# Weights split two blocks at a time, POOL normalising part of the attention weights, and a new order on TensorE, in an attention + maxout kernel

## The chip, the cores and the metric

The kernel runs on one core of a Trainium2 chip. The metric is device time in microseconds (us) of one execution; the time before is a median over three runs. The core has five engines, each of which executes its own instruction stream in order and waits on semaphores for the others: TensorE (PE in the profile; PEld is its weight load), VectorE (DVE), ScalarE (ACT), GpSimd (POOL) and SyncE (SP, which here only issues transfers).

## The reference

Sliding-window attention with a linear distance bias, then a dense maxout layer and an output projection:

```python
scores = q @ k.T / 8                                   # 8 batches, 8 heads, 576 positions, head size 64
scores = where(0 <= i - j < 128, scores - slope[h] * |i - j|, -1e9)
attn   = exp(scores - max); attn /= attn.sum(-1) + 1e-9
x      = (attn @ v)  as 4608 tokens x 512
h      = maximum(x @ w1, x @ w2, x @ w3)               # 512 -> 768 each
out    = h @ w_out                                     # 768 -> 512
```

q, k and v are float32. The four weight matrices arrive as float64 and are given to the kernel as pairs of 32-bit words.

## The kernel before

**Attention.** The eight batches are worked through in tasks, one per batch and pair of heads (32 tasks), and each task in five steps of up to 128 query rows (160 steps). A step belongs to a pair of steps, for which the work on TensorE is issued together. `products` (line 259) multiplies q and k for two steps into the score banks; `score` masks (lines 274, 277), adds the bias and takes the row minimum on DVE (line 289), and takes exp with its row sum on ACT (line 293). `sums_of` makes the reciprocals of the row sums on DVE (lines 302, 305), `normalise` multiplies each p by them on ACT (line 312), `turn` transposes p on TensorE (line 321), ACT copies the transposes out (lines 325, 331, 334), POOL cuts them to the triangles of the window (lines 335, 339), and `mix` multiplies them with v (line 361). `turn` comes LAG_T = 4 steps behind the products, `mix` LAG_X = 6 steps.

**Dense layers.** They go by a scheme with seven products of half-size blocks in place of eight (like Strassen's). Every operand is a sum or difference of blocks, split into a high and a low part in the fp32r type (ACT casts the high part, DVE or POOL subtracts to get the low one), and each product is three matmuls: low by high, high by low, high by high. A *unit* (lines 510 to 519) is one such product: 6 matmuls of 128x288 for the first layer, 9 for the output layer. There are 11 groups per batch (nine for the maxout layer, two for the output) of seven units each, 77 units per batch. A product's result stays in one of three banks of accumulators, is copied out by ACT (line 519) or combined by DVE (lines 459 to 476), and further products are accumulated on top of it in the same bank, so that the copy must be done before the bank's next product. `factors_h` forms the differences and splits of the maxout result (DVE `sub`, line 391; ACT cast, line 387; POOL subtraction, line 388).

**Weights.** In the first batch the float64 words of each of the 12 groups of weights are converted to float32 on ACT and DVE (lines 136 to 144), four sums are made (line 158), and seven blocks of 128x256 are split into high and low part (lines 168, 169). The nine groups of the maxout layer are written to DRAM (`keep`) and from the second batch on are read back through a ring of two groups, issued from POOL's queue (line 221). The three groups of the output layer stay in SBUF (`ow`).

**Order.** Every piece of work is an event with a time in steps; `at` collects them, and they are issued in order of that time. Within a step: mix, then turn, then products, then the units due. A scheduler then orders each engine's instructions by this order and by when it takes operands to be ready, so that instructions can be pulled ahead of others. `weights` is called in each step and each unit of batch 0 and advances the preparation.

## Time and profile before

| | |
|---|---|
| median of three runs | 850.38 us (847.42 to 852.41) |
| profiled execution | 846.03 us, of which the span from first to last instruction is 844.3 us |
| PE busy | 780.3 us (92%), 6272 matmuls |
| DVE busy | 570.0 us (68%) |
| ACT busy | 544.5 us (64%) |
| POOL busy | 310.3 us (37%) |
| moved by DMA | 184.78 MB, 219 GB/s on the mean |

Busy time counts an engine as busy while an instruction of its own is under way; matmuls overlap, and several in flight count once. The mean duration of a matmul in a group is therefore longer than its share of the time; the pace is read from the starts of the groups in the timeline. In the timeline, a row is a stretch of like instructions on one engine: start, duration, engine, line, operation, tiles, shape, count, and in brackets idle time ahead of it with what ended it. In the windows view each stretch has, for each engine, busy us with the number of instructions, then the granted clock of TensorE as a share of full speed, the DMA share, and GB/s.

### The profile page before, as it was taken

How to read it: one execution, taken by the hardware profiler on the slowest of the kernel's cores; microseconds unless marked ns; L12 is line 12 of the kernel's file. 1: busy time of each engine (PE TensorE's matmuls, PEld its weight loads, DVE VectorE, ACT ScalarE, POOL GpSimd, SP SyncE). 2: the span in 40 equal slices, each digit the busy share in tenths (PEclk: the TensorE clock that was granted, in tenths of full speed). 3: DMA queues.
4: the chain of work that ended last, by engine and by line, in shares of the span. 5: the costliest groups of instructions: out<-in, count | busy, mean ns of one | idle time of the engine just before them, and what ended most of it. 6: DMA issues, size and time to landing. Idle time of an engine off the chain costs nothing.

```text
span 844.3 us, 17942 instructions
## 1 busy us (share of the span) xinstructions
PE 780.3 (92%) x6272; PEld 674.3 (80%) x6272; DVE 570.0 (68%) x1830; ACT 544.5 (64%) x1790; POOL 310.3 (37%) x544
## 2 busy tenths in 40 slices
PE   4767778799999999999999999999999999999997
PEld 2335666589888988888888988889888988889897
DVE  5788989996666845775557845775657846583552
ACT  6898888876666856676556756675657756642332
POOL 1212141442354415452345415451345415440431
PEclk9865989799999999999999999999999999999999
DMA  6742568673887558873787558873787557764851
GB/s 230 278 168 70 220 230 305 210 257 125 262 277 249 195 171 261 277 253 118 239 273 252 196 175 267 275 255 110 245 281 240 194 187 244 230 223 153 296 205 56
DMA packets 43401, 184.78 MB, mean 219 GB/s; under 512 B 4784, under 2 KB 13744, under 8 KB 34096
## 3 DMA queue, kind: packets, MB, share of 16 engines
q0 software_dynamic: 18144, 115.61, 41.7%
q1 hardware_dynamic: 25024, 67.97, 22.8%
q8 instruction: 49, 0.80, 0.4%
q14 instruction: 40, 0.33, 0.1%
q10 hardware_dynamic: 144, 0.07, 0.0%
HBM read 157.68 MB, written 25.95 MB: 217 GB/s over the span
## 4 chain that ended last, share of the span: by engine, by line
PE 68%; DVE 8%; issue 8%; POOL 6%; ACT 6%; DMA 3%; SPq 0%; POOLq 0%; ACTq 0%; DVEq 0%
PE ps_m L510 53%; PE ps_x L361 6%; PE ps_s L259 5%; PE pt L321 4%; POOL hs L388 3%; DMA wt<-keep 2%; POOL pp L339 1%; POOL pp L335 1%; ACT p L293 1%; ACT hs L387 1%; DVE hs L158 1%; DVE t L473 1%; DMA hs<-in_w_all 1%; DVE hs L144 1%; DVE xs L388 1%
## 5 line engine op out<-in xcount | busy, mean ns | idle before, releaser
L510 PE MATMUL ps_m<-xs,wt 128*128 128x288 f32 x3024 | 440.8, 302 | 19.9 <-DVE hq L476 7.6
L510 PEld LDWEIGHTS ps_m<-xs,wt 128*128 128x128 f32 x3024 | 414.6, 191 | 46.6 <-issue 12.2
L519 ACT COPY t<-ps_m 128x288 f32<-128x288 f32 x264 | 101.2, 392 | 92.3 <-PE ps_m L510 91.9
L335 POOL TENSOR_SCALAR_AFFINE_SELECT pp<-pr 128x256 f32<-128x256 f32 (+1 forms) x128 | 53.9, 421 | 263.0 <-ACT pr L334 175.9
L510 PE MATMUL ps_m<-hs,ow 128*128 128x288 f32 x1008 | 144.5, 299 | 3.2 <-POOL hs L388 2.4
L293 ACT ACTIVATE p<-s,st 128x128 f32<-128x128 f32 (+1 forms) x320 | 126.7, 399 | 27.9 <-DVE st L289 27.2
L510 PEld LDWEIGHTS ps_m<-hs,ow 128*128 128x128 f32 x1008 | 136.0, 188 | 9.6 <-POOL hs L388 5.9
L388 POOL TENSOR_TENSOR hs<-hq,hs 128x288 fp32r<-128x288 f32 x112 | 101.3, 914 | 88.3 <-ACT hs L387 88.1
L221 POOL DMA_DIRECT2D wt<-keep x126 | 69.8, 554 | 150.3 <-PE ps_m L510 148.8
L312 ACT ACTIVATE p<-p,st 128x128 f32<-128x128 f32 (+1 forms) x320 | 108.6, 399 | 20.6 <-DVE st L305 20.0
L289 DVE CUSTOM_DVE_ANT_0 s<-ps_s,bias 128x128 f32<-128x128 f32 (+1 forms) x300 | 77.5, 283 | 25.9 <-PE ps_s L259 19.0
L473 DVE TENSOR_TENSOR t<-ps_m,t 128x288 f32<-128x288 f32 x144 | 65.1, 453 | 43.5 <-PE ps_m L510 27.3
L361 PE MATMUL ps_x<-pp,v 128*64 128x256 f32 (+3 forms) x768 | 85.6, 338 | 7.3 <-POOL pp L335 6.6
L277 DVE COPY_PREDICATED ps_s<-prev,ps_s 128x256 f32<-128x256 uint8 x120 | 50.6, 421 | 56.9 <-PE ps_s L259 55.7
L259 PE MATMUL ps_s<-qk 64*64 64x192 f32 (+1 forms) x1080 | 71.3, 346 | 11.5 <-DVE st L289 7.4
L321 PE MATMUL pt<-ident,p 128*128 128x128 f32 (+1 forms) x320 | 62.0, 295 | 17.3 <-ACT p L312 15.2
L387 ACT CAST hs<-hq 128x288 fp32r<-128x288 f32 x120 | 50.3, 433 | 39.0 <-DVE hq L474 26.0
L361 PEld LDWEIGHTS ps_x<-pp,v 128*64 128x64 f32 (+1 forms) x768 | 46.7, 140 | 35.1 <-POOL pp L335 11.8
L321 PEld LDWEIGHTS pt<-ident,p 128*128 128x128 f32 (+1 forms) x320 | 37.2, 145 | 42.7 <-ACT p L312 20.9
L474 DVE TENSOR_TENSOR hq<-t,hq 128x288 f32<-128x288 f32 x144 | 67.4, 475 | 2.7
L259 PEld LDWEIGHTS ps_s<-qk 64*64 64x64 f32 x1080 | 40.1, 141 | 26.9 <-issue 13.2
L293 ACT ACTIVATION_READ_ACCUMULATOR p<-s,st 128x1 f32 (+1 forms) x320 | 61.5, 192 | 0.0
(56 smaller groups left out, 719.2 us busy)
## 6 DMA issues: line engine op xcount, KB each, us to landing
wt<-keep POOLq DMA_DIRECT2D x63, 1024.0 KB, 7.2
wt<-keep POOLq DMA_DIRECT2D x63, 768.0 KB, 4.6
qk<-in_qk SPq DMA_DIRECT2D x31, 576.0 KB, 5.8
hs<-in_w_all SPq DMA_DIRECT2D x24, 512.0 KB, 6.6
v<-in_v SPq DMA_DIRECT2D x32, 320.0 KB, 4.8
keep<-wt SPq DMA_DIRECT2D x9, 1024.0 KB, 4.7
outT<-t SPq DMA_DIRECT2D x64, 144.0 KB, 1.8
keep<-wt SPq DMA_DIRECT2D x9, 768.0 KB, 5.2
```

The source lines that it names most:

```text
L221: nc.gpsimd.dma_start(wts[n, a], keep[n % 9][a])
L259: nc.tensor.matmul(ps[j][d:d + D, o:o + k1 - k0], lhsT=qkt[t][j * D:(j + 1) * D, 0, q0:q0 + D], rhs=qkt[t][j * D:(j + 1) * D, 1, k0:k1], s ...
L289: nc.vector.tensor_tensor_reduce(out=s[:n], in0=ps[j][:n, P:2 * P], in1=(bias if i else bias0)[:n, 2 * hp + j, :], scale=-0.125, scalar=3. ...
L293: nc.scalar.activation(p[:n, j], s[:n], AF.Exp, bias=st[:n, 0, a, j:j + 1], scale=-1.0, accum_out=st[:n, 1, a, j:j + 1])
L312: nc.scalar.activation(p[:n, j], p[:n, j], AF.Copy, scale=st[:n, 2, a, j:j + 1])
L321: nc.tensor.transpose(out=pt[:, a, j, :n], in_=p[:n, j], identity=ident[:n, :n])
L361: nc.tensor.matmul(x[j * D:(j + 1) * D, c:c + e - a], lhsT=vv[:n, i, j * D:(j + 1) * D], rhs=w[:n, j].rearrange("p a b -> p (a b)")[:, a:e ...
L388: e.tensor_tensor(out=lo, in0=src, in1=hi.bitcast(F32), op=ALU.subtract)
L473: nc.vector.tensor_tensor(out=s, in0=ps, in1=e, op=ALU.add)
L474: nc.vector.tensor_tensor(out=h, in0=s, in1=h, op=ALU.max)
L510: nc.tensor.matmul(ps, lhsT=lt, rhs=rt, start=i == 0 and k in (0, 1, 4), stop=i == len(pairs) - 1, skip_group_check=True,)
L519: nc.scalar.copy(out=e, in_=ps)
```

## The change

Five things change, and nothing that is computed.

1. *Splitting of weights.* The four sums are written so that two neighbouring blocks lie behind each other; blocks 0 and 1, 2 and 3, and 4 and 6 are then split with one ACT cast and one DVE subtraction of 128x512 each, block 5 alone with 128x256. So 84 casts and 84 subtractions become 48 and 48 (36 of twice the width). `ow` becomes one tile in place of seven. The pace of the preparation goes from 2 of 10 pieces per call to 1.4 of 7.
2. *Normalising.* In the first two batches every other p is normalised by one POOL multiplication of 128x256 in place of two ACT instructions of 128x128: 20 POOL instructions more and 40 ACT instructions fewer.
3. *Attention order.* Within a step the work is issued as mix, products, turn instead of mix, turn, products, and mix and products stand at the head of the step.
4. *Differences.* In `factors_h`, the differences that are formed last are issued two or five units later.
5. *Pinning.* From step 50 on, matmuls and transposes keep on TensorE the order in which they are issued; the scheduler no longer moves them there.

```diff
-    ow = [const.tile([P, 3, 2, W], F32R, name=f"ow{k}") for k in range(7)]
+    ow = const.tile([P, 7, 3, 2, W], F32R, name="ow")
...
-            (s1, a10, a11, ALU.add), (s2, s1, a00, ALU.subtract), (s4, a01, s2, ALU.subtract),
-            (s3, a00, a10, ALU.subtract),
+            (h0[:, a], l0[:, a], l0[:, b], ALU.subtract), (l0[:, b], l0[:, b], l1[:, b], ALU.add),
+            (h1[:, a], l0[:, b], l0[:, a], ALU.subtract), (h1[:, b], l1[:, a], h1[:, a], ALU.subtract),
...
-    def part(g, k):
-        src = blocks(g)[k]
+    def part(g, n):
+        (l0, h0), (l1, h1) = [[x.bitcast(F32) for x in words(g, j)] for j in range(2)]
+        src = (l0, h1, l1, h0[:, :W])[n]
...
-        nc.scalar.copy(out=t[:, 0], in_=src)
-        nc.vector.tensor_tensor(out=t[:, 1], in0=src, in1=t[:, 0].bitcast(F32), op=ALU.subtract)
+        t = t[:, (slice(0, 2), slice(2, 4), slice(4 - k, 7 - k, 2), 5 - k)[n]]
+        if n < 3:
+            src = src.rearrange("p (k n) -> p k n", k=2)
+            hi, lo = t[:, :, 0], t[:, :, 1]
+        else:
+            hi, lo = t[:, 0], t[:, 1]
+        nc.scalar.copy(out=hi, in_=src)
+        nc.vector.tensor_tensor(out=lo, in0=src, in1=hi.bitcast(F32), op=ALU.subtract)
...
+    def pe(ins):
+        if fixed:
+            tc.keep_in_program_order(ins)
...
         for a, p in enumerate(two):
+            if t < 2 * NP and (t + a) % 2 == 0:
+                nc.gpsimd.tensor_tensor(
+                    out=p[:n], in0=p[:n], in1=st[:n, 2, a].unsqueeze(2).broadcast_to([n, 2, P]), op=ALU.mult
+                )
+                continue
             for j in range(2):
                 nc.scalar.activation(p[:n, j], p[:n, j], AF.Copy, scale=st[:n, 2, a, j:j + 1])
...
         elif ij == (1, 1):
             t = hq["t", p]
+            when += 2 * (p < 2)
...
             later(when, cut, 4, b10)
+            when += 5 if p < 2 else 2
             later(when, sub, b10, b10, t)
...
-                weights(2, 10 * g_order.index(g) + 4 + k)
+                weights(1.4, 7 * g_order.index(g) + 4 + (0, 0, 1, 1, 2, 3, 2)[k])
...
-                at(c + LAG_T + 0.02, turn, t * NB + i)
-                at(c + 0.03, products, t * NB + i)
+                at(c + 0.002, products, t * NB + i)
+                at(c + LAG_T + 0.003, turn, t * NB + i)
...
-            at(e - e % 2 + shift[b] + LAG_X + 0.01, mix, t, i)
+            at(e - e % 2 + shift[b] + LAG_X + 0.001, mix, t, i)
...
+    at(2 * n_steps + LAG_X + shift[2], fix)
```

What this moves is seen in the instruction streams. In these rows a line number is that of the kernel that the row belongs to: units are line 510 before and 529 after, products (tile `ps_s`) 259 and 271, transposes (`pt`) 321 and 338, mix (`ps_x`) 361 and 378.

TensorE, a pair of steps in the middle of a batch (the same place in every batch from the third on), before:

```order
L510 MATMUL ps_m_6189<-xs,wt_6040 128x288 x6
L361 MATMUL ps_x<-pp,v 64x256 x4
L510 MATMUL ps_m_6132<-xs,wt_6040 128x288 x6
L321 MATMUL pt<-ident,p 128x128 x2
L321 MATMUL pt<-ident,p 128x64 x2
L259 MATMUL ps_s<-qk 64x192 x8
L510 MATMUL ps_m_6246<-xs,wt_6068 128x288 x6
```

and now:

```order
L529 MATMUL ps_m_6091<-xs,wt_5942 128x288 x6
L378 MATMUL ps_x<-pp,v 64x256 x4
L271 MATMUL ps_s<-qk 64x192 x8
L338 MATMUL pt<-ident,p 128x128 x2
L338 MATMUL pt<-ident,p 128x64 x2
L529 MATMUL ps_m_6031<-xs,wt_5942 128x288 x6
```

The transposes now stand between the products and the units, in every pair of steps from there on; and the one unit that stood between mix and transposes here has gone behind them.

TensorE, the pair of steps ahead of that one, before:

```order
L361 MATMUL ps_x<-pp,v 64x256
L510 MATMUL ps_m_5882<-xs,wt_5809 128x288 x6
L510 MATMUL ps_m_6005<-xs,wt_5856 128x288 x6
L510 MATMUL ps_m_6016<-xs,wt_5856 128x288 x6
L510 MATMUL ps_m_6074<-xs,wt_5919 128x288 x6
L361 MATMUL ps_x<-pp,v 64x256
L361 MATMUL ps_x<-pp,v 64x128 x2
L361 MATMUL ps_x<-pp,v 64x64 x4
L321 MATMUL pt<-ident,p 128x128 x4
L259 MATMUL ps_s<-qk 64x128 x4
L259 MATMUL ps_s<-qk 64x192 x4
```

and now:

```order
L378 MATMUL ps_x<-pp,v 64x256 x2
L378 MATMUL ps_x<-pp,v 64x128 x2
L378 MATMUL ps_x<-pp,v 64x64 x4
L271 MATMUL ps_s<-qk 64x128 x4
L271 MATMUL ps_s<-qk 64x192 x4
L338 MATMUL pt<-ident,p 128x128 x4
```

The first matmul of mix no longer stands four units ahead of the others: the four units come before all of mix.

DVE, where the last difference of the first third of a batch's maxout (`hq<-hq,t`, line 391 before, 408 after) meets the first combinations of the next (lines 476 and 495), before:

```order
L391 TENSOR_TENSOR hq<-hq,t 128x288
L476 TENSOR_TENSOR hq<-ps_m_5666,t 128x288
L476 TENSOR_TENSOR hq<-ps_m_5754,t 128x288
L302 TENSOR_SCALAR st<-st 64x2
L476 TENSOR_TENSOR hq<-ps_m_5655,t 128x288
L305 RECIPROCAL st<-st 64x2
```

and now:

```order
L314 TENSOR_SCALAR st<-st 64x2
L317 RECIPROCAL st<-st 64x2
L408 TENSOR_TENSOR hq<-hq,t 128x288
L495 TENSOR_TENSOR hq<-ps_m_5560,t 128x288
L495 TENSOR_TENSOR hq<-ps_m_5652,t 128x288
L495 TENSOR_TENSOR hq<-ps_m_5549,t 128x288
```

The reciprocals of the row sums have moved ahead; the difference, which is issued later in the program, still stands ahead of the three combinations.

More of the change, by code (lines that the diff above doesn't have):

```diff
@@ L144, in convert, with sums @@
         nc.vector.tensor_tensor(out=lf, in0=lf, in1=hw, op=ALU.mult)
-    def blocks(g):
+    def sums(g):
         (l0, h0), (l1, h1) = [[x.bitcast(F32) for x in words(g, j)] for j in range(2)]
         a, b = slice(0, W), slice(W, 2 * W)
-        return l0[:, a], h0[:, b], h1[:, a], h1[:, b], l1[:, a], h0[:, a], l1[:, b], l0[:, b]
-    def sums(g):
-        a00, s1, s2, s4, a01, s3, a11, a10 = blocks(g)
         for out, x, y, op in (
-            (s1, a10, a11, ALU.add), (s2, s1, a00, ALU.subtract), (s4, a01, s2, ALU.subtract),
-            (s3, a00, a10, ALU.subtract),
+            (h0[:, a], l0[:, a], l0[:, b], ALU.subtract), (l0[:, b], l0[:, b], l1[:, b], ALU.add),
+            (h1[:, a], l0[:, b], l0[:, a], ALU.subtract), (h1[:, b], l1[:, a], h1[:, a], ALU.subtract),
         ):
             nc.vector.tensor_tensor(out=out, in0=x, in1=y, op=op)
-    def part(g, k):
-        src = blocks(g)[k]
+    def part(g, n):
+        (l0, h0), (l1, h1) = [[x.bitcast(F32) for x in words(g, j)] for j in range(2)]
+        src = (l0, h1, l1, h0[:, :W])[n]
         if g < 9:
-            if k in (0, 4):
-                place(g, k // 4)
-            t = wts[g, k // 4][:, k % 4]
-        else:
-            t = ow[k][:, g - 9]
-        nc.scalar.copy(out=t[:, 0], in_=src)
-        nc.vector.tensor_tensor(out=t[:, 1], in0=src, in1=t[:, 0].bitcast(F32), op=ALU.subtract)
-        if g < 9 and k in (3, 6):
-            nc.sync.dma_start(keep[g][k // 4], wts[g, k // 4].bitcast(F32))
+            if n in (0, 2):
+                place(g, n // 2)
+            t, k = wts[g, n // 2], n // 2 * 4
+        else:
+            t, k = ow[:, :, g - 9], 0
+        t = t[:, (slice(0, 2), slice(2, 4), slice(4 - k, 7 - k, 2), 5 - k)[n]]
[6 more added lines that the diff above has]
+        nc.vector.tensor_tensor(out=lo, in0=src, in1=hi.bitcast(F32), op=ALU.subtract)
+        if g < 9 and n in (1, 3):
+            nc.sync.dma_start(keep[g][n // 2], wts[g, n // 2].bitcast(F32))
     def place(n, a):
@@ L191, in preparing @@
             yield
-            for k in range(7):
-                while g < 9 and not ahead(g, k // 4):
+            for k in range(4):
+                while g < 9 and not ahead(g, k // 2):
                     yield True
@@ L198, in preparing @@
                 fetch(g_order[n + 2])
-    prepared = 0
+    prepared, owed = 0, 0
     steps_of_weights = preparing()
     def weights(n=0, upto=0):
-        nonlocal prepared
-        while n > 0 or prepared < upto:
+        nonlocal prepared, owed
+        owed += n
+        while owed >= 1 or prepared < upto:
             stuck = next(steps_of_weights, True)
             if stuck:
-                assert prepared >= upto or prepared == 120, (prepared, upto)
+                assert prepared >= upto or prepared == 84, (prepared, upto)
+                owed = 0
                 return
             prepared += 1
-            n -= 1
+            owed = max(0, owed - 1)
     streamed = 18
@@ L218, in stream @@
         n, a = divmod(streamed, 2)
-        if n < 9 * B and prepared == 120 and ahead(n, a):
+        if n < 9 * B and prepared == 84 and ahead(n, a):
             place(n, a)
@@ L263, in products @@
                         start=True, stop=True, skip_group_check=True,
-                    )
+                    ))
     def score(t, i):
@@ L320, in turn @@
             for j in range(2):
-                nc.tensor.transpose(out=pt[:, a, j, :n], in_=p[:n, j], identity=ident[:n, :n])
+                pe(nc.tensor.transpose(out=pt[:, a, j, :n], in_=p[:n, j], identity=ident[:n, :n]))
         r = s_p.tile([P, 2, 2, P], F32, name="pr", bufs=2)
@@ L360, in mix @@
             for j in range(2):
-                nc.tensor.matmul(
+                pe(nc.tensor.matmul(
                     x[j * D:(j + 1) * D, c:c + e - a],
@@ L509, in unit @@
         for i, (lt, rt) in enumerate(pairs):
-            nc.tensor.matmul(
+            pe(nc.tensor.matmul(
                 ps, lhsT=lt, rhs=rt, start=i == 0 and k in (0, 1, 4), stop=i == len(pairs) - 1,
                 skip_group_check=True,
-            )
+            ))
         if g < 9:
@@ L569, in attention_maxout_kernel, with fix @@
     for s in range(1, n_steps + LAG_X):
-        at(s + 0.2, weights, 2)
+        at(s + 0.2, weights, 1.4)
+    def fix():
+        nonlocal fixed
+        fixed = True
+    at(2 * n_steps + LAG_X + shift[2], fix)
     load(0)
```

7 lines of the change are left out of this document (4 added, 3 removed).

## The prediction

> **What bounds the kernel now.** I read the busy times by stretch first (us of PE, PEld, DVE, ACT and POOL, each with its instructions, then the granted clock).
>
> ```profile
> 20.00:80.00 60.00, 43.30 (x266) 21.91 (x265) 50.07 (x194) 54.41 (x183) 13.75 (x30) 0.68 0.51 184
> 80.00:200.00 120.00, 101.87 (x753) 83.97 (x752) 112.59 (x344) 97.98 (x304) 37.68 (x57) 0.89 0.65 231
> 200.00:790.00 590.00, 579.65 (x4853) 518.22 (x4852) 374.72 (x1203) 363.74 (x1223) 239.10 (x422) 1.00 0.68 224
> ```
>
> There are two kernels in one. To 200 us the weights are prepared beside the first two batches: from 20 to 80 us ACT is the fullest (54.41 of 60), from 80 to 200 us DVE (112.59 of 120), and TensorE runs at a reduced clock (0.68, 0.89). From 200 to 790 us TensorE is busy for 579.65 of 590 us at full clock while DVE, ACT and POOL have room. There only fewer or cheaper boundaries on TensorE save time. So I read its timeline next, over three pairs of steps of one batch.
>
> ```profile
> 411.21 1.08 PE L361 MATMUL ps_x<-pp,v 128*64 128x256 f32 x8
> 412.22 0.70 PE L321 MATMUL pt<-ident,p 128*128 128x128 f32 x4
> 412.86 0.88 PE L259 MATMUL ps_s<-qk 64*64 64x192 f32 x16
> 413.67 6.66 PE L510 MATMUL ps_m<-xs,wt 128*128 128x288 f32 x48
> 420.25 1.25 PE L361 MATMUL ps_x<-pp,v 128*64 128x256 f32 x16
> ...
> 430.87 0.60 PE L321 MATMUL pt<-ident,p 128*128 128x128 f32 x4
> 431.40 0.88 PE L259 MATMUL ps_s<-qk 64*64 64x192 f32 x16
> ...
> 441.25 3.47 PE L510 MATMUL ps_m<-xs,wt 128*128 128x288 f32 x24
> 444.65 0.65 PE L361 MATMUL ps_x<-pp,v 128*64 128x256 f32 x2
> 445.22 3.45 PE L510 MATMUL ps_m<-xs,wt 128*128 128x288 f32 x24
> 448.61 1.24 PE L361 MATMUL ps_x<-pp,v 128*64 128x256 f32 x14
> 449.78 0.66 PE L321 MATMUL pt<-ident,p 128*128 128x128 f32 x4
> 450.36 0.77 PE L259 MATMUL ps_s<-qk 64*64 64x128 f32 x16
> 451.07 5.86 PE L510 MATMUL ps_m<-xs,wt 128*128 128x288 f32 x42
> 456.86 1.08 PE L361 MATMUL ps_x<-pp,v 128*64 128x256 f32 x8
> 457.88 1.06 PE L510 MATMUL ps_m<-xs,wt 128*128 128x288 f32 x6
> 458.78 0.65 PE L321 MATMUL pt<-ident,p 128*128 128x128 f32 x4
> 459.35 0.88 PE L259 MATMUL ps_s<-qk 64*64 64x192 f32 x16
> 460.16 5.86 PE L510 MATMUL ps_m<-xs,wt 128*128 128x288 f32 x42
> ```
>
> From start to start, 42 unit matmuls take 5.79 us (451.07 to 456.86) and 24 take 3.40: 18 in 2.39, so 0.133 each, and 0.21 per stretch for getting in and out. The transposes between mix and products take 0.64 (412.22 to 412.86) or 0.58 (449.78 to 450.36). What they cost between units is seen once in the early part, at full clock:
>
> ```profile
> 172.56 0.27 PE L321 MATMUL pt<-ident,p 128*128 128x128 f32 x1
> 172.58 0.51 PE L510 MATMUL ps_m<-xs,wt 128*128 128x288 f32 x2
> 172.93 0.27 PE L321 MATMUL pt<-ident,p 128*128 128x128 f32 x1
> ...
> 183.01 1.19 PE L361 MATMUL ps_x<-pp,v 128*64 128x256 f32 x14
> 183.96 0.38 PE L259 MATMUL ps_s<-qk 64*64 64x192 f32 x2
> ```
>
> One transpose and two unit matmuls take 0.37 (172.56 to 172.93); less 2 x 0.133 that is 0.10 for the transpose. Transposes and units use the array in one shape (128\*128), and next to each other they pay no boundary.
>
> **The change on TensorE, from 200 us.** *Products ahead of transposes.* Four transposes beside units cost 0.42, against 0.58 to 0.64 behind mix: 0.19 saved on the mean, if mix to products costs what mix to transposes did, and products to transposes what products to units did. Per batch seven of the ten pairs have mix directly ahead: 7 x 0.19 = 1.33. Where units stand ahead (430.87 to 431.40, 0.53), the 0.11 saved comes back as the boundary between units and products: nothing. The attention of the later batches fills some 545 us from 200 us on, and a batch takes 94.5 us (the stall below comes at 333.12 and at 427.57), so 5.8 batches: 7.7 us. *Mix in one piece.* The two early mix matmuls cost 0.57 (444.65 to 445.22) and break 48 units into 24 and 24 (3.40 + 3.39 against 6.58 at 413.67, so 0.21), while the fourteen left are under way as long as sixteen elsewhere (1.24 against 1.25): 0.78. *The lone unit.* From mix to mix the piece now takes 1.02 + 0.90 + 0.57 + 0.81 + 5.79 = 9.09; in the new order 1.02 + 0.81 + 0.42 + 6.58 = 8.83: 0.26. These two come in five batches: 5.2 us. Together 12.9 us.
>
> One wait stays.
>
> ```profile
> PE ps_m L510 <- DVE hq L476: 7.0, 5, 1.4
> ...
> 333.12 3.46 PE L510 MATMUL ps_m<-xs,wt 128*128 128x288 f32 x24 [1.41 <-DVE hq L476]
> ...
> 427.57 3.46 PE L510 MATMUL ps_m<-xs,wt 128*128 128x288 f32 x24 [1.40 <-DVE hq L476]
> ```
>
> The first row is a wait of 200 to 790 us (total, times, longest): TensorE stands 1.4 us once in each of five batches, for a combination on DVE that is queued behind the last difference, which itself waits for POOL to have read its input. The change issues that difference five units later, but DVE's stream still has it ahead of the three combinations, and POOL's operations ahead of it are the same. I count nothing for it, and take 5 x 0.2 off, since what the pair of steps ahead of the stall saves is waited away there. That leaves **-12 us**. The bounds: if the boundary only moves, the first part is lost and -4 remains; if mix to products is almost free, as where fourteen mix matmuls take 0.95 (183.01 to 183.96) against 1.17, another 0.22 x 7 x 5.8 = 9 is won: -21. On the far side, ACT's copies of finished products may now stand behind exps that start earlier; a new wait of 0.2 us in each of 58 pairs would give 12 back, so 0 is the other end.
>
> By the Trainium skill ("TensorEngine Tiling (Array Packing)", section Tiling Modes) every change of tiling mode drains the array; by that rule mix to products (128x64 to 64x64) stays a paid boundary and transposes to units none. The 0.10 agrees with it; by the rule alone the sum is the -12, and -21 isn't reached.
>
> **The change up to 200 us.** The costs:
>
> ```profile
> L312 ACT ACTIVATE p<-p,st 128x128 f32<-128x128 f32 (+1 forms) x320 | 108.6, 399 | 20.6 <-DVE st L305 20.0
> L388 POOL TENSOR_TENSOR hs<-hq,hs 128x288 fp32r<-128x288 f32 x112 | 101.3, 914 | 88.3 <-ACT hs L387 88.1
> L169 DVE TENSOR_TENSOR wt<-hs,wt 128x256 fp32r<-128x256 f32 x63 | 26.8, 443 | 2.3 <-ACT wt L168 2.1
> L168 ACT CAST wt<-hs 128x256 fp32r<-128x256 f32 x63 | 25.4, 429 | 6.3 <-DVE hs L158 4.7 <-DVE hs L144 0.8 <-PE ps_x L361 0.3
> L144 DVE TENSOR_TENSOR hs<-hs 128x512 f32<-128x512 f32 x24 | 16.6, 708 | 0.6 <-ACT hs L140 0.6
> L136 ACT ACTIVATE hs<-hs 128x512 int32<-128x512 uint32 x24 | 15.8, 679 | 2.3 <-DMA hs<-in_w_all 2.3
> ```
>
> Splits on DVE: 84 x 0.425 (26.8 / 63) = 35.7 before; 36 x 0.69 (16.6 / 24) + 12 x 0.425 = 30.0 now: -5.7. On ACT 84 x 0.403 = 33.9 becomes 36 x 0.66 + 12 x 0.403 = 28.5: -5.4. Normalising takes 40 x 0.339 (108.6 / 320) = 13.6 off ACT and puts 20 x 0.80 (101.3 / 112, scaled from 288 to 256 elements) = 16 on POOL, which is busy for 51 of 180 us here. What this costs DVE:
>
> ```profile
> 408.68 0.46 DVE L474 TENSOR_TENSOR hq<-t,hq 128x288 f32<-128x288 f32 x1
> ...
> 418.78 0.81 POOL L388 TENSOR_TENSOR hs<-hq,hs 128x288 fp32r<-128x288 f32 x1 [1.62 <-ACT hs L387]
> 419.13 0.78 DVE L474 TENSOR_TENSOR hq<-t,hq 128x288 f32<-128x288 f32 x1
> ```
>
> The same DVE operation takes 0.46 alone and 0.78 beside a POOL operation. All 20 POOL operations beside such a one would add 6.4 us to DVE; I take half, as much of DVE's work reads PSUM: 3.2. DVE's net is then -2.5, ACT's -19.
>
> From 20 to 80 us lie about 25 steps, so five of the eight tasks with 13 of the 20 p, and five of the twelve weight groups: ACT loses 8.8 + 2.3, DVE nothing net. DVE's 50.07 become the fullest; filled as ACT was (0.907) they need 55: -5 at most. From 80 to 200 us DVE's net -2.5 at its filling of 0.94 gives -2.6 at most. I take **-3** of these 7.6, since here the end passes from engine to engine and a freed one often waits. The ends are -8, and +9: DVE slowed by the full 6.4 (net +0.7), and each of the 20 p held 0.4 us by another POOL operation on its path.
>
> By the Trainium skill ("GPSIMD Engine Reference", section Key points) POOL shares its SBUF interfaces with DVE and collides with DVE instructions that have two SBUF inputs, which speaks against this part. The 0.78 agrees. By the rule every weight operation beside POOL is hit, the -3 becomes about 0, and the time 838.
>
> **The sum.** 846.03 (profiled execution: span 844.3 and 1.7 around it) - 12 - 3 = 831. The profiled execution lies 4.35 under the median of the runs, so the forecast for the median is **835 us**.
>
> **Rivals.** *The boundary only moves* (-4 - 3): 843. For it: products to transposes is a change of shape too. Against: one fewer change per pair remains. *POOL's queue holds the transposes*: a p normalised on POOL stands in one in-order queue with cuts that wait for ACT.
>
> ```profile
> POOL pp L335 <- ACT pr L325: 62.7, 19, 12.5
> ```
>
> The longest such wait is 12.5 us. If half of the 20 p come 2.5 us late, the transposes, and with them the products behind them on TensorE and DVE's next scores, wait 25 us: 850.4 - 15 + 25 = 860. It decides from about 1 us per p on. Against: a transpose comes four steps behind its scores. *Everything pays* (-21 - 8, on the median): 821. *No net change*: new waits for ACT and DVE behind the pinned order give back the 12, and the early part gives nothing: 850.
>
> **How the numbers follow.** A measurement of this kernel tells about 0.5% (4.25 us) from no change: faster is under 846.1, slower over 854.6. The forecast gets 0.60 (0.57 faster, 0.03 same), the moved boundary 0.15 (0.11, 0.04), POOL's queue 0.12 (0.02 same, 0.10 slower), everything pays 0.08 (faster), no net change 0.05 (0.04 same, 0.01 slower). Together faster 0.76, same 0.13, slower 0.11. The forecast's own range is 826 to 845; with the cases on either side until two in ten are left out, 822 to 850.
>
> **What would show it.** Right: behind 200 us, rows of 16 products followed by 4 transposes, and 0.45 or less from these to the units; mix rows of 8 and 16 alone; a batch of about 92 us from stall to stall in place of 94.5, and the stall of 1.4 us still there; 200 us reached 3 us earlier with ACT clearly emptier and DVE as full. Wrong: transposes behind products that take 0.6 again, TensorE waiting for `t` of ACT's copies after each pair, or transposes that wait for POOL before 200 us.

## The result, and the profile after

The changed kernel takes **836.05 us** (median of 4 runs, 835.39 to 837.38), against 849.24 us for the kernel before (4 runs beside it, 847.42 to 852.41): a ratio of 0.9843, 95% interval 0.9808 to 0.9877, 13.2 us less. Its profiled execution took 836.26 us, span 834.6; that of before 846.03, span 844.3. So from trace to trace 9.7 us are to be explained, 3.5 fewer than from median to median.

The busy times by stretch of the kernel after (columns as in the prediction's first view):

```profile
20.00:80.00 60.00, 42.28 (x266) 21.79 (x264) 51.63 (x180) 48.01 (x151) 24.42 (x42) 0.64 0.58 199
80.00:200.00 120.00, 101.42 (x735) 84.95 (x735) 110.46 (x318) 88.86 (x252) 46.71 (x64) 0.88 0.62 222
200.00:780.00 580.00, 568.85 (x4865) 515.57 (x4863) 366.32 (x1206) 363.00 (x1231) 233.23 (x423) 1.00 0.69 229
```

ACT is emptier up to 200 us (48.01 and 88.86 against 54.41 and 97.98) and POOL fuller; DVE stays as full as it was (51.63 and 110.46 against 50.07 and 112.59). Behind 200 us TensorE is still the bound.

Two marks cut the span in three: the start of the first unit, and the start of the first output layer (tile `ow`), with which the first batch's dense layers end. The timeline of TensorE before:

```profile
74.42 3.25 PE L510 MATMUL ps_m<-xs,wt 128*128 128x288 f32 x12 [0.31 <-DVE xs L388]
...
184.84 2.68 PE L510 MATMUL ps_m<-hs,ow 128*128 128x288 f32 x18
```

and after, with the same marks, then the stalls of two neighbouring batches and the last stall:

```profile
69.98 1.68 PE L529 MATMUL ps_m<-xs,wt 128*128 128x288 f32 x6
...
186.24 2.68 PE L529 MATMUL ps_m<-hs,ow 128*128 128x288 f32 x18
...
333.11 3.46 PE L529 MATMUL ps_m<-xs,wt 128*128 128x288 f32 x24 [1.36 <-DVE hq L495]
...
425.12 3.46 PE L529 MATMUL ps_m<-xs,wt 128*128 128x288 f32 x24 [1.35 <-DVE hq L495]
...
701.25 3.47 PE L529 MATMUL ps_m<-xs,wt 128*128 128x288 f32 x24 [1.36 <-DVE hq L495]
```

The first unit starts 4.4 us earlier, yet the first output layer 1.4 us later: from the one to the other 116.3 us instead of 110.4. At the first stall both kernels stand level (333.11 against 333.12), so the 1.4 us are won back between 186 and 333. Then each batch takes 92.0 us from stall to stall (333.11 to 425.12) in place of 94.45 (333.12 to 427.57): 2.42 us in each of four batches, 9.7 in all. Behind the last stall both need the same (834.6 - 701.25 = 133.35; 844.3 - 710.93 = 133.37).

Pairs of steps from two neighbouring batches in TensorE's timeline after, with the stretch that mix used to break (438.62) and the one that held the lone unit (453.48):

```profile
400.04 1.19 PE L378 MATMUL ps_x<-pp,v 128*64 128x256 f32 x14
400.98 0.33 PE L271 MATMUL ps_s<-qk 64*64 64x128 f32 x2
401.06 0.23 PE L378 MATMUL ps_x<-pp,v 64*64 64x64 f32 x2
401.12 0.71 PE L271 MATMUL ps_s<-qk 64*64 64x128 f32 x14
401.76 0.66 PE L338 MATMUL pt<-ident,p 128*128 128x128 f32 x4
402.17 6.64 PE L529 MATMUL ps_m<-xs,wt 128*128 128x288 f32 x48
408.74 1.08 PE L378 MATMUL ps_x<-pp,v 128*64 128x256 f32 x8
409.76 0.88 PE L271 MATMUL ps_s<-qk 64*64 64x192 f32 x16
410.57 0.70 PE L338 MATMUL pt<-ident,p 128*128 128x128 f32 x4
411.20 6.67 PE L529 MATMUL ps_m<-xs,wt 128*128 128x288 f32 x48
...
428.51 0.88 PE L271 MATMUL ps_s<-qk 64*64 64x192 f32 x16
...
429.74 6.68 PE L529 MATMUL ps_m<-xs,wt 128*128 128x288 f32 x48
...
436.34 1.08 PE L378 MATMUL ps_x<-pp,v 128*64 128x256 f32 x8
...
438.16 0.70 PE L338 MATMUL pt<-ident,p 64*128 64x64 f32 x4
438.62 7.02 PE L529 MATMUL ps_m<-xs,wt 128*128 128x288 f32 x48
445.57 1.19 PE L378 MATMUL ps_x<-pp,v 128*64 128x256 f32 x14
...
453.48 1.08 PE L378 MATMUL ps_x<-pp,v 128*64 128x256 f32 x8
...
462.53 1.19 PE L378 MATMUL ps_x<-pp,v 128*64 128x256 f32 x14
```

The order is as the change says: products, transposes, units. Where the prediction saw one price for every pair there are three. With 16 mix matmuls, mix to units takes 2.13 us (400.04 to 402.17) against 2.46 before (448.61 to 451.07 in the prediction's lines). Mix runs into the products: the second mix row (64\*64) stands in the middle of the products, which have the same array shape, and the transposes need 0.41 (401.76 to 402.17). With 8 mix matmuls the same way takes 2.46 (408.74 to 411.20), as it did before (411.21 to 413.67): there the last two of the four transposes have 64 rows, and the transposes need 0.63 to the units. Where the first two have 64 rows instead (the row at 438.16 bears the shape of its first transpose, 64\*128), the transposes need 0.46, and mix to units takes 2.28 (436.34 to 438.62) against 2.45 at the same place of a batch before:

```profile
344.35 1.08 PE L361 MATMUL ps_x<-pp,v 128*64 128x256 f32 x8
...
346.80 3.47 PE L510 MATMUL ps_m<-xs,wt 128*128 128x288 f32 x24
```

TensorE's waits from 200 to 780 us (total, times, longest) are the same as before in their first place, and small otherwise:

```profile
PE ps_m L529 <- DVE hq L495: 6.8, 5, 1.4
PE ps_m L529 <- ACT t L538: 1.5, 2, 1.2
```

One small wait of each batch is gone, and the prediction doesn't speak of it. In the output layer TensorE used to stop for a result of POOL (`hs`). Before:

```profile
377.27 3.65 PE L510 MATMUL ps_m<-hs,ow 128*128 128x288 f32 x24
381.13 1.86 PE L510 MATMUL ps_m<-hs,ow 128*128 128x288 f32 x12 [0.22 <-POOL hs L388]
382.83 0.60 PE L321 MATMUL pt<-ident,p 128*128 128x128 f32 x4
```

and after:

```profile
375.94 5.13 PE L529 MATMUL ps_m<-hs,ow 128*128 128x288 f32 x36
381.00 0.88 PE L271 MATMUL ps_s<-qk 64*64 64x192 f32 x16
```

The 36 matmuls take 5.06 us to the next stretch in place of 5.56.

### The profile page after: what moved, and what is told of

It is laid out like the page before. It is cut to its first block, busy times and chain, and to the rows that moved or that the text cites. A ratio compares the mean times of both kernels' runs of the same rounds, so it can differ in the third digit from the quotient of the medians.

```text
span 834.6 us, 17886 instructions
## 1 busy us (share of the span) xinstructions
PE 769.1 (92%) x6272; PEld 672.6 (81%) x6272; DVE 560.9 (67%) x1794; ACT 528.2 (63%) x1714; POOL 326.0 (39%) x564
## 4 chain that ended last, share of the span: by engine, by line
PE 68%; DVE 12%; POOL 7%; ACT 6%; issue 5%; DMA 2%; SPq 0%; POOLq 0%; ACTq 0%; DVEq 0%
PE ps_m L529 53%; PE ps_x L378 7%; PE ps_s L271 5%; POOL hs L405 4%; PE pt L338 4%; DVE t L492 2%; ACT p L305 2%; DMA hs<-in_w_all 1%; DVE wt L173 1%; DVE hq L493 1%; DVE s L301 1%; POOL pp L352 1%; POOL pp L356 1%; DVE ps_s L289 1%; POOL p L324 1%
## 5 line engine op out<-in xcount | busy, mean ns | idle before, releaser
L529 PE MATMUL ps_m<-hs,ow 128*128 128x288 f32 x1008 | 142.7, 298 | 3.0 <-POOL hs L405 1.2
L352 POOL TENSOR_SCALAR_AFFINE_SELECT pp<-pr 128x256 f32<-128x256 f32 (+1 forms) x128 | 56.6, 442 | 208.4 <-ACT pr L351 121.7
L405 POOL TENSOR_TENSOR hs<-hq,hs 128x288 fp32r<-128x288 f32 x112 | 95.2, 858 | 89.0 <-ACT hs L404 85.3
L227 POOL DMA_DIRECT2D wt<-keep x126 | 70.1, 556 | 118.4 <-PE ps_m L529 117.6
L329 ACT ACTIVATE p<-p,st 128x128 f32<-128x128 f32 x280 | 97.1, 396 | 16.6 <-DVE st L317 16.2
L271 PE MATMUL ps_s<-qk 64*64 64x192 f32 (+1 forms) x1080 | 68.8, 337 | 8.9 <-DVE st L301 4.8
L338 PEld LDWEIGHTS pt<-ident,p 128*128 128x128 f32 (+1 forms) x320 | 35.2, 145 | 49.8 <-issue 20.7
L493 DVE TENSOR_TENSOR hq<-t,hq 128x288 f32<-128x288 f32 x144 | 70.1, 490 | 2.8
L351 ACT COPY pr<-pt 128x256 f32<-128x256 f32 x64 | 19.0, 321 | 73.7 <-PE pt L338 73.6
```

The source lines that it names most:

```text
L227: nc.gpsimd.dma_start(wts[n, a], keep[n % 9][a])
L271: pe(nc.tensor.matmul(ps[j][d:d + D, o:o + k1 - k0], lhsT=qkt[t][j * D:(j + 1) * D, 0, q0:q0 + D], rhs=qkt[t][j * D:(j + 1) * D, 1, k0:k1] ...
L329: nc.scalar.activation(p[:n, j], p[:n, j], AF.Copy, scale=st[:n, 2, a, j:j + 1])
L338: pe(nc.tensor.transpose(out=pt[:, a, j, :n], in_=p[:n, j], identity=ident[:n, :n]))
L405: e.tensor_tensor(out=lo, in0=src, in1=hi.bitcast(F32), op=ALU.subtract)
L493: nc.vector.tensor_tensor(out=h, in0=s, in1=h, op=ALU.max)
```

## The experiments

The labels stand for the kernels. "Batch 1" in an expectation is the first of the eight batches. All were timed in three rounds beside the kernel before; ratios are against it. The kernel before took 848.67 to 850.08 us beside them, so that a difference of 1 us between two rows says little. The marks are those of each kernel's trace; "batch" is the time from stall to stall, and in the three kernels with the edit of e7_diff_last, where the stall is gone, from output layer to output layer of the third to sixth batch.

| kernel | us | ratio, 95% interval | first unit | first output layer | batch |
|---|---|---|---|---|---|
| before | 849.24 | | 74.4 | 184.8 | 94.45 |
| the change | 836.05 | 0.9843 (0.9808 to 0.9877) | 70.0 | 186.2 | 92.0 |
| e1_order_only | 839.06 | 0.9863 (0.9836 to 0.9890) | 75.2 | 186.0 | 92.36, one 93.9 |
| e5_no_pin | 838.59 | 0.9886 (0.9858 to 0.9915) | 70.1 | 185.0 | 92.37, one 93.9 |
| e4_turn_first | 841.81 | 0.9917 (0.9889 to 0.9945) | 71.4 | 185.4 | 93.1 |
| e7_diff_last | 830.06 | 0.9776 (0.9743 to 0.9810) | 69.8 | 186.4 | 91.3 to 92.0 |
| e2_no_pool_norm | 840.42 | 0.9885 (0.9858 to 0.9912) | 79.7 | 188.8 | 92.0 |
| e6_pool_norm_b0 | 832.27 | 0.9806 (0.9766 to 0.9846) | 70.3 | 182.7 | 92.0 |
| e3_narrow_split | 834.64 | 0.9817 (0.9790 to 0.9844) | 72.2 | 182.0 | 92.0 to 93.5 |
| e9_pairs_narrow | 842.87 | 0.9914 (0.9880 to 0.9947) | 76.2 | 190.7 | 92 to 93.6 |
| e10_wide_early | 840.44 | 0.9889 (0.9860 to 0.9918) | 70.9 | 188.9 | 92.0 |
| e12_pace | 835.63 | 0.9849 (0.9833 to 0.9866) | 79.3 | 185.5 | 92.0 |
| e11_three | 830.43 | 0.9795 (0.9772 to 0.9817) | 73.9 | 185.3 | 90.4 to 92.1 |
| e14_wide_two | 827.76 | 0.9752 (0.9727 to 0.9777) | 70.5 | 183.5 | 90.4 to 91.3 |

A scale for the early marks: e5_no_pin has the same order on TensorE as the change up to there, and its output layer begins 1.2 us earlier. Differences of about 1 us between two traces at this mark say nothing.

### TensorE's order: e1_order_only, e5_no_pin, e4_turn_first

The order of attention alone, put into the kernel before (no fixed order behind step 50, no later differences, no split, no POOL):

```diff
-                at(c + LAG_T + 0.02, turn, t * NB + i)
-                at(c + 0.03, products, t * NB + i)
+                at(c + 0.002, products, t * NB + i)
+                at(c + LAG_T + 0.003, turn, t * NB + i)
...
-            at(e - e % 2 + shift[b] + LAG_X + 0.01, mix, t, i)
+            at(e - e % 2 + shift[b] + LAG_X + 0.001, mix, t, i)
```

> The kernel before with the attention order alone (mix, products, turn); no pinning, old weights, old normalising, old differences. Theory (the gain is TensorE's boundaries): a batch from stall to stall takes 92.8 us (92.0 as in the changed kernel plus 0.78 for the two early mix matmuls, which stay without pinning), the output layer of batch 1 begins within 2 us of the 184.8 of before, and the time is 849.2 - 1.65 x 5.8 = 840. Rival (pinning makes the gain): a batch still takes 94.4 and the time is 849.

Its stalls, from the timeline:

```profile
518.78 3.46 PE L510 MATMUL ps_m<-xs,wt 128*128 128x288 f32 x24 [1.35 <-DVE hq L476]
...
611.15 3.45 PE L510 MATMUL ps_m<-xs,wt 128*128 128x288 f32 x24 [1.34 <-DVE hq L476]
```

92.37 us apart, so the order alone gives 2.1 of the 2.42 us. The theory holds, and the rival, that fixing the order on TensorE is what pays, falls. The other side of this, the change without the fixed order:

```diff
-        if fixed:
+        if False:
```

> The change without the fixed order on TensorE behind the second batch. Theory, the fixed order is worth the 0.33 us per batch by which the order alone (92.36) fell short of the change (92.03): the two mix matmuls go ahead again, batch 92.4, 837.7 us. Rival, the later differences gave that, not the fixed order: batch 92.0, 836 us.

```profile
424.30 3.46 PE L529 MATMUL ps_m<-xs,wt 128*128 128x288 f32 x24 [1.34 <-DVE hq L495]
...
441.17 0.65 PE L378 MATMUL ps_x<-pp,v 128*64 128x256 f32 x2
...
516.67 3.45 PE L529 MATMUL ps_m<-xs,wt 128*128 128x288 f32 x24 [1.36 <-DVE hq L495]
```

The two mix matmuls go ahead of the others again and break the 48 units, and the batch is at 92.37 (424.30 to 516.67): the theory's 92.4. So mix in one piece is worth 0.34 us per batch and no more, and the later differences give nothing here. (One batch of e5_no_pin took 93.9; the granted clock was 0.89 over 15 us of it. One of e1_order_only did too, with 0.91 over 18 us.)

The change with only transposes and products exchanged again:

```diff
-                at(c + 0.002, products, t * NB + i)
-                at(c + LAG_T + 0.003, turn, t * NB + i)
+                at(c + LAG_T + 0.002, turn, t * NB + i)
+                at(c + 0.003, products, t * NB + i)
```

> The changed kernel with turn again ahead of products within a step; pinning and the rest stay. Theory (the order saves 0.19 per pair of steps with mix ahead, 1.33 a batch, and pinning the 0.78 of the early mix matmuls): a batch takes 92.0 + 1.4 = 93.4, the early part as in the changed kernel, time 836 + 8 = 844. Rival (the boundary only moves, pinning does it all): a batch takes 92.0, time 836.

```profile
427.12 2.66 PE L529 MATMUL ps_m<-xs,wt 128*128 128x288 f32 x18 [0.63 <-DVE st L317]
...
520.24 2.66 PE L529 MATMUL ps_m<-xs,wt 128*128 128x288 f32 x18 [0.61 <-DVE st L317]
```

93.12 per batch, 1.1 more than the change, where 1.4 was expected; the time 841.81. The wait is shorter here (0.63 instead of 1.35), so part of what the old order costs is hidden in the stall. Added up row by row over a batch, the stretches between one run of units and the next (mix, transposes and products) take 1.9 us more than in the change, and the output layer 0.5 more, where the wait for POOL's `hs` is back (0.19 in its row); 1.2 of these 2.4 us are saved again around the stall. So the wait for `hs` goes with products ahead of transposes. What brings POOL's result forward there isn't traced.

### The stall: e7_diff_last

The last difference, which stands ahead of the three combinations in DVE's stream, is forced behind the third of them:

```diff
-            later(when, sub, b10, b10, t)
+            later(when, last if p < 2 else sub, b10, b10, t)
...
+    combined = []
+
+    def last(out, x, y):
+        with tc.issue_after(combined[-1]):
+            sub(out, x, y)
```

(`combined` collects the additions of line 495.)

> The changed kernel with the last difference of the first two thirds of the maxout forced behind the three combinations on DVE that it stood ahead of (an order of issue on DVE, nothing else). Theory (TensorE's stall of 1.35 us per batch is that difference waiting for POOL): the stall is gone, a batch takes 90.7 us in place of 92.0, time 836 - 6.7 = 829. Rival (another wait takes its place, as for the next thirds' results): a batch takes 91.5 to 92, time 834 to 836.

The longest of TensorE's waits from 200 to 780 us in this kernel, and one of its times in the timeline:

```profile
PE ps_m L535 <- DMA wt<-keep: 4.4, 4, 1.4
```

```profile
523.22 4.23 PE L535 MATMUL ps_m<-xs,wt 128*128 128x288 f32 x30 [1.42 <-DMA wt<-keep]
```

The waits for `hq`, 6.8 us in the change, are gone, so the difference was their cause, as the prediction read it. But in this trace a batch goes from 92.0 to between 91.3 and 92.0 only: a few rows later TensorE now stands up to 1.4 us for weights that are still being read back from DRAM. The mechanism is the theory's, the period is nearer to the rival's: one wait took the place of the other.

It doesn't always do so. This trace was the slowest of its four runs (833.55; the others 828.8 to 830.2): its span is only 2.8 us below the change's (831.8), the median 6.0. And e14_wide_two, which is e6_pool_norm_b0 (92.0 a batch) with this edit, has two neighbouring output layers

```profile
369.11 2.66 PE L535 MATMUL ps_m<-hs,ow 128*128 128x288 f32 x18
...
459.49 2.66 PE L535 MATMUL ps_m<-hs,ow 128*128 128x288 f32 x18
```

90.4 us apart, and another two as well; the batch between them takes 91.3 and holds a wait of 0.76 for the weights. e11_three shows the same: 90.4 twice, and 92.1 with a wait of 1.47. So the edit is worth 1.6 us in a batch whose weights come in time. How many batches of the faster runs of e7_diff_last were of this kind isn't shown.

### POOL's share: e2_no_pool_norm, e6_pool_norm_b0

All normalising back on ACT, all else as in the change:

```diff
-            if t < 2 * NP and (t + a) % 2 == 0:
-                nc.gpsimd.tensor_tensor(
-                    out=p[:n], in0=p[:n], in1=st[:n, 2, a].unsqueeze(2).broadcast_to([n, 2, P]), op=ALU.mult
-                )
-                continue
```

> The changed kernel with all p normalised on ACT. Theory (POOL's share relieves ACT up to 75 us and slows DVE afterwards, so it is worth nothing on the whole): first unit back near 74 us, the output layer of batch 1 begins at 184 to 186 us, a batch takes 92.0 as now, time 834 to 836. Rival A (it pays): the output layer of batch 1 begins at 190, time 840. Rival B (it costs the 5.8 us lost between first unit and output layer): it begins at 181, time 831.

The two marks in its timeline:

```profile
79.70 1.81 PE L524 MATMUL ps_m<-xs,wt 128*128 128x288 f32 x6 [1.80 <-DVE xs L400]
...
188.79 2.87 PE L524 MATMUL ps_m<-hs,ow 128*128 128x288 f32 x18
```

No theory gave the shape of it. POOL's share brings the first unit 9.7 us ahead (79.70 to 69.98), far more than expected, and then costs 7 us on the way to the output layer (109.1 us here, 116.3 in the change). Net it pays 4.4 us (840.42 against 836.05), which is nearest to the rival that it pays. Then the same with POOL in the first batch alone:

```diff
-            if t < 2 * NP and (t + a) % 2 == 0:
+            if t < NP and (t + a) % 2 == 0:
```

> The changed kernel with POOL normalising in the first batch only (10 p in place of 20). With none on POOL the first unit came at 79.7 us in place of 70.0, but from there to the output layer of batch 1 it took 109 us in place of 116. Theory (POOL pays ahead of the first unit, where ACT is full, and costs behind it, where DVE is full and shares the access with POOL): first unit at 71, output layer of batch 1 at 182, time 832. Rival (the early gain is waited away later whoever normalises, since the weights set the pace there): first unit at 71, output layer at 186, time 836.

```profile
182.67 2.86 PE L529 MATMUL ps_m<-hs,ow 128*128 128x288 f32 x18
```

In its marks it is as the theory had it: the first unit stays early (70.3), the output layer comes 3.6 us earlier than in the change, and the time is 832.27. With the weights split two blocks at a time, the ten p of the first batch bring the gain, and the ten of the second batch take part of it back.

What POOL's share costs DVE is seen when the weights' operations on DVE are compared from 4 to 192 us. In the change, with POOL's own 128x256 multiplication from the grouping over the whole span:

```profile
L173 DVE TENSOR_TENSOR wt<-hs,wt 128x512 fp32r<-128x512 f32 (+1 forms) x36 | 24.0, 679 | 3.6 <-ACT wt L172 3.2
...
L155 DVE TENSOR_TENSOR hs<-hs 128x256 f32<-128x256 f32 x36 | 17.1, 475 | 0.0
...
L324 POOL TENSOR_TENSOR p<-p,st 128x256 f32<-128x256 f32 x16 | 13.3, 831 | 56.8 <-DVE st L317 43.9 <-ACT wt L172 8.7 <-DVE st L301 2.7
```

and without POOL's share (e2_no_pool_norm):

```profile
L173 DVE TENSOR_TENSOR wt<-hs,wt 128x512 fp32r<-128x512 f32 (+1 forms) x36 | 23.8, 671 | 3.9 <-ACT wt L172 3.7
...
L155 DVE TENSOR_TENSOR hs<-hs 128x256 f32<-128x256 f32 x36 | 15.8, 439 | 0.0
```

All seven groups of weight operations together are busy for 100.2 us in the kernel before, 97.7 without POOL's share and 101.3 in the change. So the wider splits save 2.5 us of DVE (4.0 in the splits themselves, 35.3 to 31.3, of which 1.5 comes back in other rows), and POOL's 20 multiplications give 3.6 us back. The narrow split beside POOL's share (e3_narrow_split) takes 103.8, so both prices come out the same the other way round. But POOL's price doesn't go by the number of its multiplications: with the ten of the first batch alone (e6_pool_norm_b0) the groups take 100.6, only 0.7 less than with twenty. So the 3.6 us by which the output layer comes earlier there isn't seen as DVE time, and the reason that the theory of e6_pool_norm_b0 gives, DVE slowed behind the first unit, isn't shown.

### The split: e3_narrow_split, e9_pairs_narrow, e10_wide_early

The change with the split of before, one block at a time:

```diff
-                weights(1.4, 7 * g_order.index(g) + 4 + (0, 0, 1, 1, 2, 3, 2)[k])
+                weights(2, 10 * g_order.index(g) + 4 + k)
...
-        at(s + 0.2, weights, 1.4)
+        at(s + 0.2, weights, 2)
```

(with `ow`, `sums` and `part` as before the change)

> The changed kernel with the weights split one block at a time, as before. Theory (5.7 us of DVE and 5.4 of ACT work saved, worth about half): the output layer of batch 1 begins at 189 in place of 186.2, time 839. Rival (two blocks at a time come late for the units that need them, and that is the loss after 75 us): it begins at 183, time 833.

```profile
181.99 2.65 PE L526 MATMUL ps_m<-hs,ow 128*128 128x288 f32 x18
```

The theory that the new split as a whole pays falls: with the one of before the output layer comes 4.2 us earlier and the time is 834.64, 1.4 less than the change, with overlapping intervals of the two ratios. (In its trace 2.1 of the 4.2 us are lost again in two batches of 93.5 and 92.6 us, the first with a granted clock of 0.89 over 16 us.) The edit also puts back the seven tiles of `ow`, the old places of the blocks and the old pace; these weren't tried apart. Why should fewer instructions cost time? Two attempts to tell. First, the pairs and their pace kept, but each pair split by two narrow instructions per engine:

```diff
-        nc.scalar.copy(out=hi, in_=src)
-        nc.vector.tensor_tensor(out=lo, in0=src, in1=hi.bitcast(F32), op=ALU.subtract)
+        each = [(hi[:, c], lo[:, c], src[:, c]) for c in range(2)] if n < 3 else [(hi, lo, src)]
+        for x, y, z in each:
+            nc.scalar.copy(out=x, in_=z)
+            nc.vector.tensor_tensor(out=y, in0=z, in1=x.bitcast(F32), op=ALU.subtract)
```

> The changed kernel with each pair of blocks split by two narrow casts and subtractions in place of one wide one, in the same pieces and at the same pace. Splitting one block at a time had brought the output layer of batch 1 to 182.0 from 186.2. Theory A (the wide instructions themselves: they stand longer in ACT's and DVE's queues ahead of what TensorE waits for): output layer of batch 1 at 182 to 183, time 834. Theory B (the pace in pieces of two blocks: more is done at once): it stays at 186 or comes later by the 5 us of work that the wide form saves, 188, time 838.

842.87, the first unit 6 us later than in the change and the output layer at 190.7: it isn't the wide instruction itself that costs. This kernel differs from the change in that instruction alone and is 4.4 us later at the output layer, so the wide instruction pays, as theory B has it, and by more than that theory's 188 and 838. What is better in e3_narrow_split can only lie in what else its edit changes. Second, wide pairs in the five groups ahead of the first unit only, one block at a time later:

```diff
-            for k in range(4):
+            for k in range(4 if n < 5 else 7):
...
-                part(g, k)
+                part(g, k) if n < 5 else part_one(g, k)
```

(`part_one` is the split of one block as before; the pace is 1.4, then 2)

> The changed kernel with two blocks at a time only in the five groups of weights that are split before the first unit, and one block at a time, at the old pace, in the seven others. Theory (the wide split pays 2 us ahead of the first unit and costs 6 behind it): first unit at 70, output layer of batch 1 at 180, time 831. Rival (the gain ahead is waited away behind the first unit, as the weights set the pace): output layer at 182, as with one block at a time everywhere, time 834.5.

840.44, the output layer at 188.9. Both theories fall: mixing the two is worse than either alone.

### The pace of the weights: e12_pace

Two pieces of preparation offered in each step instead of 1.4:

```diff
-        at(s + 0.2, weights, 1.4)
+        at(s + 0.2, weights, 2)
```

> The change, but the weights are offered two pieces of preparation in each step of attention instead of 1.4, so they stand earlier in every engine's order. Theory, the preparation of the weights sets the pace from the first unit to the first output layer: preparation ends near 172 instead of 176 us, the first output layer begins near 182 instead of 186.2, 832 us; the first unit may come up to 2 us later than 70.0. Rival, DVE's and ACT's time itself is the limit and the pieces only push scores back: first unit at 73 or later, first output layer at 186 or later, 836 to 838.

The first unit starts 9.3 us later than in the change (79.3), and the output layer (185.5) within the 1.2 us that two traces of one order differ by; the time is 835.63 against 836.05. The last split of weights starts at 175.4 us, against 176.2 in the change, not at 172. The theory that the pace of the offers holds the stage up falls; that pieces offered earlier only push the first units back is what the trace shows. It also shows that the first unit's start says little of the end of this stage.

### Together: e11_three, e14_wide_two

Three edits together, and the same without the narrow split:

```diff
-            if t < 2 * NP and (t + a) % 2 == 0:
+            if t < NP and (t + a) % 2 == 0:
...
-            later(when, sub, b10, b10, t)
+            later(when, last if p < 2 else sub, b10, b10, t)
```

(e14_wide_two; e11_three has the split of e3_narrow_split besides)

> The change with three edits together: one block at a time split (e3_narrow_split), POOL normalises in the first batch only (e6_pool_norm_b0), the last difference behind the three combinations (e7_diff_last). Theory, the three act in different places and their gains add: -1.4 - 3.8 - 6.0 from 836.05, so 825 us; first output layer at 180 us, batch 92.0. Rival, the split and the normalising relieve the same waits between 75 and 180 us, so only the larger of the two counts: 826.5 to 828, first output layer at 182.5.

> The change with POOL normalising in the first batch only and the last difference behind the three combinations, weights split two blocks at a time as in the change. Compared with e11_three only the split differs. Theory, splitting two blocks at a time costs as it did in e3_narrow_split: 1.4 us above e11_three, 826.3, first output layer at 182.7. Rival, two blocks at a time cost only where POOL normalises beside it: not above e11_three, 825 or less, first output layer not later than there.

The first output layer in e11_three, then in e14_wide_two:

```profile
185.34 2.87 PE L532 MATMUL ps_m<-hs,ow 128*128 128x288 f32 x18
```

```profile
183.45 2.84 PE L535 MATMUL ps_m<-hs,ow 128*128 128x288 f32 x18
```

e11_three takes 830.43, more than either expectation (825, 826.5 to 828): the gains don't add. e14_wide_two takes 827.76 (824.22 to 829.71), 8.3 less than the change and the fastest kernel here; the edits to POOL's share and to the difference add nearly in full (-3.8 and -6.0 would give 826.3). Its absolute numbers are those of its theory, but the comparison is the rival's: splitting two blocks at a time is now 2.7 us faster than one (the ranges of the two just touch: 829.25 to 833.91 in e11_three), where it was 1.4 slower with POOL in both batches. POOL's share turns its sign in the same way. With the wide split, taking POOL out of the second batch brings the first output layer from 186.2 to 182.7 (183.5 in e14_wide_two); with the narrow split it goes from 182.0 to 185.3. Each of the two edits alone gains about 4 us at this mark, and both together about 1. Neither has a price of its own that these runs agree on.

## Why the prediction was right, and where not

The median, 835 forecast and 836.05 measured, came closer than the sum, and that is in part luck. The sum was 831 for a profiled execution, which took 836.26; the 4.35 us by which the profiled execution of before lay under its median made up for it, and that distance didn't recur (836.26 against 836.05). Trace against trace, the forecast was -15 and the measurement -9.7: -11.1 from the first output layer on (659.5 to 648.4 us) and +1.4 ahead of it.

*TensorE from 200 us: -12 forecast, -11.1 measured.* Right in sum, and the mechanism is shown by e1_order_only, where the order alone takes 11.0 us off the 850.08 of the kernel before beside it, and by e4_turn_first. But its terms were sized wrongly, one was missing, and the errors cancel: that too is luck.

- *Products ahead of transposes*, forecast 1.33 a batch: 1.9 in the rows. The 0.19 for seven pairs alike was wrong: the four pairs with 16 mix matmuls gain 0.33, of the four with 8 the two whose transposes begin with 64 rows gain 0.17 and the two whose transposes end with them nothing, and the two pairs without mix, counted at nothing, gain 0.11 (1.34 before, from 430.87 to 432.21; 1.23 now, from 428.51 to 429.74). Counted by the array shapes of the rows, the way from mix to units has two changes of shape fewer than before where 0.33 is gained, one fewer where 0.17 is, and none fewer where nothing is; the 0.11 isn't told by this count. The bound "mix to products almost free" was true for half of the pairs with mix; the prediction named it and took the other value.
- *The wait for POOL's `hs`* in the output layer, not in the sum: 0.5 a batch.
- *Mix in one piece*, forecast 0.78: 0.34 (e5_no_pin). The 48 units behind it take 6.95 (438.62 to 445.57), not 6.58.
- *The lone unit*, forecast 0.26: 0.04. From mix to mix the piece takes 9.05 (453.48 to 462.53) in place of 9.09. The working had its four transposes at 0.42; the last two have 64 rows, and the four take 0.63.
- *The pair of steps ahead of the stall*: what it saves is waited away, as the prediction had it, but that is 0.33 and not 0.2. The units ahead of the stall, with the stall, take 4.86 before (422.71 to 427.57) and 5.19 now (419.93 to 425.12). All five together make 2.45 a batch, where 2.42 is measured.
- *Number of batches*: forecast 5.8 and 5. A full 2.42 came in four batches, and 1.4 between 186 and 333 us, where mix stood in one piece and no lone unit was there before either. Behind the last stall nothing was left: the way to the last output layer is 0.6 us shorter, and TensorE then waits 1.06 us for POOL's `hs` in place of 0.46.

*The stall stays*: right, 1.35 us where it was 1.4. Its cause was read rightly too (e7_diff_last), and removing it is worth its 1.4 us, with some 0.2 more, in a batch whose weights come in time (90.4 against 92.0); in a batch that waits for weights from DRAM half of that or all is lost (91.3 and 92.1).

*Up to 200 us: -3 forecast, +1.4 measured.* Half right, and the step failed in its second half.

- *From 20 to 80 us*, at most -5: the first unit came 4.4 us earlier. That is right, and POOL's share is needed for it: without it (e2_no_pool_norm) the first unit comes 5.3 us later than before. It isn't enough, since with the same share and another pace (e12_pace) the first unit comes 4.9 later than before. But the sum carried the gain to the end, and the trace shows it spent before the first output layer. Later first units with an equal or earlier output layer (e3_narrow_split, e12_pace) say the same.
- *From 80 to 200 us*, at most -2.6, from a net DVE of -2.5: the weights' operations on DVE became 1.1 us longer (100.2 to 101.3). POOL's cost to DVE, 3.2 forecast, is 3.6; the split's saving, 5.7 forecast, is 4.0 in its rows and 2.5 net. So DVE had no less to do, and this part of the gain had lost its ground. The far end, DVE at +0.7, was the right one. On POOL the 20 multiplications took 19.9 us, not 16: 13.3 for the 16 of full height, and 6.6 for the four of 64 rows.
- The Trainium skill ("GPSIMD Engine Reference", section Key points) says that POOL and DVE share SBUF interfaces and get in each other's way where DVE reads two SBUF inputs. The trace agrees in kind: 36 of the 48 sums (line 155) take 475 ns on the mean with POOL's share and 439 without. The prediction's "-3 becomes about 0" by that rule was closer than its own -3.

What remains open is why the output layer comes between 182.0 and 190.7 us in these kernels. Busy time doesn't tell: the narrow split has more DVE work and gets there 4.2 us sooner, and with POOL in one batch only the sign turns. It is a chain that passes from engine to engine, and each edit puts other instructions next to each other. The runs show that the first batch's share on POOL pays (188.8 without any share, 182.7 with it) and that the wide instruction as such pays 4.4 us there (e9_pairs_narrow); for the second batch's share and for the split as a whole they show no stable price.

Two of the prediction's signs of being right didn't come: in two of ten pairs the transposes take 0.63 to the units, not 0.45 or less, and the end of the early part came 1.4 us later instead of 3 earlier.

*The rivals.* "The boundary only moves" falls (2.1 us a batch from the order alone). "POOL's queue holds the transposes" falls as a total, though it exists in small: up to 190 us TensorE waits 9.0 us for p of POOL, in eight waits with a longest of 3.9, against the 25 that the rival priced, and the first unit still comes early. "Everything pays" falls. Its TensorE end (-21) isn't reached, though the free passage from mix to products, which it rested on, is real in half of the pairs. "No net change" falls: ACT's copies cost TensorE 1.5 us in all behind 200 us, 0.9 before. The rule that a change of tiling mode drains the array, from the Trainium skill ("TensorEngine Tiling (Array Packing)", section Tiling Modes), agrees with the count of shape changes above, in the pairs with mix; in the 16-matmul pairs the last mix matmuls have the shape of the products (64\*64), so by the same rule no drain was due there, which the prediction overlooked when it took all of mix as 128*64.

## What to carry to other kernels

Before pricing a boundary, read the shape of the last instruction of the one stretch and of the first of the next, not the shape that names most of the stretch: here it made the difference between 0.33 us, 0.17 and nothing for the same exchange. A gain at an early mark is worth something only if the next mark moves too; in a stage where the end passes between engines, take a sum over busy times as a bound and count nothing until one engine is shown to be the last. And when a stall is to be removed, look a few rows further for the transfer that is late next: here it took back up to all that a batch would have gained, in the batches where it was late.

## What the runs showed of the hardware that was not expected

- Matmuls of one array shape run into each other: mix matmuls of 64\*64 start 0.06 to 0.08 us from the products around them (400.98, 401.06, 401.12), with no boundary between the two kinds.
- Four transposes between products and units take 0.41 us when all are 128x128 (401.76 to 402.17), 0.46 when the first two have 64 rows (438.16 to 438.62) and 0.63 when the last two have (410.57 to 411.20), though the row of the timeline shows one shape for all four.
- Twenty POOL multiplications, 0.83 us on the mean for the 16 of full height, lengthen DVE's weight operations by 3.6 us in all (97.7 to 101.3); the ten of the first batch alone by 2.9 (100.6).
